# RWKV-7 recurrence and wave mixer: masked evictions shared by three engines, decay sums partly on TensorE, v partly in 1280-byte runs, mixer tiles in pairs

## The chip, the cores and the metric

The kernel runs on one core of one Trainium2 chip. The metric is the device time of one execution in microseconds, as the median of several runs.

## The reference

Six inputs r, k, v, w, a, b of shape (4, 8, 768, 40): batch, heads, time, features per head. For every batch and head a 40x40 state is carried over 768 steps; then a mixer works on the result seen as x of shape (4, 768, 320).

```python
for t in range(S):
    y[:, :, t] = np.einsum('bhd,bhde->bhe', rt, state)
    Sa = np.einsum('bhde,bhe->bhd', state, at)
    state = state * wt[:, :, None, :] - np.einsum('bhd,bhe->bhde', Sa, bt) \
            + np.einsum('bhd,bhe->bhde', vt, kt)
...
theta = x @ w_theta
zr, zi = x * np.cos(theta), x * np.sin(theta)
u = x + np.einsum('ts,bsd->btd', w_tok_r, zr) + np.einsum('ts,bsd->btd', w_tok_i, zi)
return u + np.maximum(u @ w_ch, 0.0)
```

Inputs and output are float32; the kernel's matmuls take bfloat16.

## The kernel before, in words

**Recurrence.** Time is cut into 24 chunks of 128 steps, six for each batch element; the chunk number i runs from 0 to 23. The time steps of a chunk lie on the 128 partitions, the 8 heads x 40 features along the free dimension. Inside a chunk the recurrence is written as products of masked 128x128 score matrices; from chunk to chunk a state `gt` is carried.

- `loads(i)` issues five loads on the SP queue (w, k, b, a, v), each of 160 KB in rows of 160 bytes, since a head's 40 floats are contiguous only for one time step. r comes for two chunks at a time in runs of 1280 bytes (eight time steps in a row), and its transposition by TensorE and the two evictions `rT` (L454) restore the order.
- `prep(i)`: ScalarE takes the logarithm of w (`lw`, L382); TensorE sums it over time with a triangular matrix (L389) and sums each head's decay of the whole chunk (L391, L395); ScalarE takes the exponential (`ex`, L399). VectorE adds `lw` to the sum (`sx`, L402), the sum without the present step, and ScalarE makes `we` of it (L406). GpSimd multiplies k and b by `ex` and a by `we` (`kb` L413, `ah` L417), and casts v (L422). TensorE transposes the results, ScalarE evicts them (`kbT`, `aT`, `vT`, L342).
- `scores` (called for psi, phi, lamv and lamu): 16 matmuls of 64 rows fill two PSUM banks with 8 heads of 128x128 scores (L467). One VectorE instruction of 128x1024 multiplies them by the triangular mask on their way to SBUF (L472). There are 4 x 24 = 96 of these masked evictions.
- `recurrence(i)`: psi times v plus the state's part (L500, L506), eviction `nx` (L512), phi (L518), eviction `nu` (L522), then the new state (L539, `sum` L550, `gt` L554 or L558), and its transposition `gd`.
- `readout(i)`: the output y of the chunk from lamv, lamu and the old state (L602, L609, L611); VectorE multiplies it by `we` into the tile `x` (L618).

**Mixer.** For each x tile: three transpositions, one padded (L582), an eviction, three matmuls with w_theta (L627) and an eviction `th` (L637). When a batch element's six tiles are there, ScalarE takes sine and cosine (`cs`, L651, with a change of the activation table before and after), GpSimd multiplies them by x (`zr`, `zi`, L663). `mix_row` then makes each of the six output tiles with 12 matmuls of 320 columns (L680), adds x (`u`, L687), transposes u, multiplies by w_ch (L627) and finishes with `oo` (L696) and a store on the SP queue. The token matrices come in blocks through the GpSimd queue (L717) into four `wrow` buffers, and are transposed by TensorE (L725, L729).

**Order.** Nothing is scheduled when the program is built. Each operation is recorded by `add` with its engine, its reads and its writes; `Plan.order` emits them as the fixed list `ORDER` says, and `HOMES` gives each its PSUM bank. So the order on every engine, on SP's and GpSimd's queues too, is that of `ORDER`. Mixer work of one batch element is spread between the recurrence of the next. `WARM` puts idle matmuls on `busy` in front of a few operations at the start (L774).

```python
        out = [self.ops[n] for n in ORDER]
        homes = iter(HOMES)
        self.home = {}
        for o in out:
            if o.new is not None:
                b = next(homes)
                self.home[o.new[0]] = (b, b + 1) if o.new[1] == 2 else (b,)
```

Of the kernel before, what the change touches and what calls it, by code (L numbers as in the profile page):

```python
# [19 lines left out]
FROM_POOL = 4  # L20
ORDER = [
    0, 5, 3, 6, 2, 1, 19, 20, 4, 21, 12, 22, 23, 34, 26, 25, 80, 35, 30, 10, 31, 24, 7, 28, 79,
    29, 8, 27, 38, 36, 40, 9, 39, 32, 33, 14, 105, 41, 81, 42, 82, 13, 43, 53, 83, 15, 84, 226,
    54, 89, 55, 106, 11, 56, 107, 58, 90, 227, 57, 16, 91, 59, 37, 85, 60, 229, 62, 108, 18,
    111, 86, 64, 63, 17, 92, 65, 110, 74, 228, 68, 109, 69, 44, 114, 112, 93, 115, 70, 76, 61,
    116, 71, 135, 117, 45, 124, 113, 136, 66, 125, 137, 67, 87, 46, 138, 120, 72, 88, 94, 121,
    47, 73, 211, 95, 139, 122, 75, 126, 96, 140, 159, 143, 118, 127, 144, 160, 130, 123, 145,
    187, 161, 146, 119, 77, 188, 164, 128, 212, 162, 189, 48, 147, 213, 165, 129, 190, 163, 195,
    180, 168, 166, 196, 214, 148, 197, 131, 198, 170, 216, 191, 171, 141, 169, 217, 132, 192,
    215, 176, 174, 265, 220, 142, 78, 175, 218, 149, 199, 221, 133, 150, 266, 167, 200, 222, 49,  # L30
    172, 177, 223, 193, 267, 50, 241, 318, 230, 242, 268, 232, 173, 270, 231, 243, 269, 201,
    236, 319, 194, 244, 271, 202, 245, 320, 181, 246, 274, 219, 233, 183, 293, 275, 249, 272,
    294, 178, 182, 321, 250, 224, 295, 179, 322, 276, 97, 296, 237, 225, 251, 277, 302, 252, 98,
    203, 134, 303, 151, 456, 204, 282, 280, 286, 152, 323, 283, 297, 253, 238, 325, 254, 304,
    281, 247, 368, 255, 184, 324, 248, 298, 256, 372, 239, 327, 369, 305, 257, 299, 329, 328,
    186, 234, 273, 330, 185, 235, 258, 373, 339, 240, 457, 278, 370, 348, 340, 288, 337, 371,
    306, 458, 279, 459, 462, 343, 349, 284, 307, 502, 300, 285, 460, 350, 461, 503, 287, 351,
    308, 301, 463, 352, 504, 338, 465, 309, 289, 353, 310, 326, 466, 333, 354, 505, 311, 344,
    467, 355, 484, 468, 334, 485, 346, 471, 336, 508, 331, 472, 356, 335, 464, 345, 486, 551,
    156, 473, 332, 357, 469, 487, 552, 474, 470, 507, 488, 506, 492, 553, 374, 511, 489, 493,  # L40
    292, 554, 341, 512, 509, 290, 532, 342, 555, 358, 153, 494, 533, 513, 359, 534, 556, 495,
    514, 360, 535, 521, 361, 99, 536, 522, 496, 558, 157, 541, 347, 557, 537, 475, 377, 523,
    497, 562, 538, 158, 291, 498, 476, 499, 560, 477, 563, 510, 542, 539, 379, 500, 561, 527,
    524, 154, 540, 375, 501, 543, 376, 579, 478, 381, 544, 490, 515, 491, 566, 580, 382, 479,
    100, 516, 155, 581, 545, 383, 101, 582, 480, 396, 567, 517, 583, 568, 380, 529, 397, 546,
    518, 598, 584, 378, 398, 519, 588, 528, 569, 599, 585, 589, 399, 600, 400, 647, 530, 547,
    559, 601, 401, 520, 102, 590, 402, 525, 548, 603, 591, 586, 628, 587, 648, 602, 604, 564,
    629, 549, 526, 572, 565, 630, 605, 649, 570, 631, 607, 482, 550, 650, 653, 609, 571, 608,
    637, 483, 592, 652, 638, 481, 610, 632, 651, 593, 639, 617, 633, 578, 654, 403, 594, 640,
    656, 404, 577, 595, 52, 103, 596, 531, 205, 104, 619, 597, 618, 51, 658, 694, 641, 659, 208,  # L50
    657, 384, 642, 385, 613, 386, 620, 695, 634, 387, 696, 643, 614, 606, 644, 697, 664, 615,
    662, 709, 665, 675, 616, 388, 623, 676, 635, 389, 636, 655, 677, 206, 390, 678, 573, 660,
    207, 611, 661, 710, 663, 612, 679, 575, 712, 645, 711, 209, 680, 574, 666, 646, 210, 621,
    681, 391, 622, 405, 392, 624, 259, 684, 698, 724, 685, 262, 682, 667, 725, 686, 826, 726,
    408, 727, 409, 406, 683, 410, 687, 728, 827, 729, 393, 828, 701, 411, 625, 412, 829, 413,
    394, 699, 830, 730, 414, 705, 576, 688, 731, 700, 706, 415, 260, 395, 831, 416, 703, 689,
    626, 263, 261, 732, 365, 264, 417, 739, 733, 362, 420, 421, 315, 422, 704, 423, 424, 738,
    832, 425, 734, 690, 426, 713, 312, 691, 418, 715, 735, 692, 702, 714, 427, 835, 428, 693,
    707, 716, 833, 736, 836, 429, 708, 627, 742, 366, 737, 430, 837, 363, 367, 741, 838, 668,
    717, 747, 364, 841, 745, 854, 718, 444, 855, 671, 316, 743, 746, 445, 856, 317, 446, 740,  # L60
    719, 313, 842, 857, 447, 862, 751, 858, 847, 863, 448, 314, 744, 843, 859, 864, 669, 449,
    844, 834, 432, 749, 433, 434, 670, 872, 435, 450, 750, 436, 865, 437, 902, 849, 748, 873,
# [72 lines left out]
class Plan:  # L135
# [7 lines left out]
    def add(self, eng, kind, i, fn, cost, reads=(), writes=(), spec=None, mode=128,  # L143
            tail=0, table=None, new=None, work=0, after=()):
        o = Op()
# [45 lines left out]
def kernel(  # L191
# [91 lines left out]
    for i, t in sorted(to_zero, key=lambda e: e[0]):  # L283
        nc.vector.memset(t, 0.0)
# [526 lines left out]
```

## Time and profile before

| | |
|---|---|
| median of 3 runs | 206.35 us (206.16 to 207.54) |
| the profiled execution, its own time | 206.05 us |
| its span, first to last instruction | 204.3 us |
| busy: TensorE, VectorE, ScalarE, GpSimd | 191.4, 174.4, 151.6, 127.0 us |
| DMA packets | 134181, 30.82 MB; 125824 of them under 512 bytes |
| granted TensorE clock | 1.00 |

Busy is the time in which an engine had at least one instruction recorded as running. The records of neighbours overlap, on TensorE above all, so the busy time is more than the engine is kept for; the space from one start to the next, where nothing is waited for, tells that. The windows of the profile give the same figures for a stretch of the span, and the timeline shows single instructions with their start and duration.

### The profile page before, as it was taken

The numbers are of one execution on the slowest core, as the hardware profiler recorded it, in microseconds if no ns is written. First come the engines' busy times: TensorE is split into PE (matmuls) and PEld (weight loads), VectorE is DVE, ScalarE is ACT, GpSimd is POOL, SyncE is SP. The second block draws the span as 40 slices with busy tenths as digits, with TensorE's granted clock in tenths as the row PEclk, the third lists the DMA queues.
The fourth block names the chain that finished last, engine by engine and source line by source line (L and its number), as shares of the span: only waits on it lengthen the run. The fifth ranks groups of instructions, "written<-read, shape, count | busy, mean of one in ns | idle before, by whom it ended". The sixth has DMA issues, their size and how long they took to land.

```text
span 204.3 us, 8134 instructions
## 1 busy us (share of the span) xinstructions
PE 191.4 (94%) x3372; PEld 156.3 (77%) x3372; DVE 174.4 (85%) x277; ACT 151.6 (74%) x364; POOL 127.0 (62%) x186
## 2 busy tenths in 40 slices
PE   7878789888999999999899999999999999999993
PEld 6756668667878888887678888788888878777771
DVE  7499899799999998996886989999999987956543
ACT  3577668799999977868667859898999967756021
POOL 3015178559999996659959918548987953635000
PEclk9999999999999999999999999999999999999999
DMA  6989899999899999979999889797999400012223
GB/s 135 198 158 197 155 172 167 182 159 195 139 186 204 155 256 191 147 141 178 170 191 207 169 176 186 169 181 131 220 199 192 96 3 5 0 67 78 87 77 116
DMA packets 134181, 30.82 MB, mean 151 GB/s; under 512 B 125824, under 2 KB 134144, under 8 KB 134144
## 3 DMA queue, kind: packets, MB, share of 16 engines
q1 hardware_dynamic: 131712, 27.54, 68.8%
q0 software_dynamic: 2432, 2.77, 8.6%
q8 instruction: 26, 0.43, 0.9%
q14 instruction: 11, 0.09, 0.1%
HBM read 29.13 MB, written 3.93 MB: 162 GB/s over the span
## 4 chain that ended last, share of the span: by engine, by line
PE 71%; DVE 8%; DMA 8%; SPq 5%; ACT 2%; issue 2%; POOL 1%; DVEq 0%; ACTq 0%; POOLq 0%
PE ps_s L680 19%; PE ps_s L339 12%; PE ps_d L467 10%; PE ps_s L627 9%; SPq L358 4%; DMA wrow_i<-in_moe_w_tok_i_dram 4%; PE ps_s L582 4%; DMA raw_v<-in_v_dram 3%; PE ps_s L450 2%; PE ps_s L539 2%; DMA raw_r<-in_r_dram 2%; PE ps_s L518 2%; PE ps_s L611 2%; PE ps_s L725 2%; PE ps_s L506 2%
## 5 line engine op out<-in xcount | busy, mean ns | idle before, releaser
L413 POOL TENSOR_TENSOR kb<-raw_kb,ex 128x320 bf16<-128x320 f32 x44 | 37.6, 868 | 10.0 <-ACT ex L399 4.3
L680 PE MATMUL ps_s<-zr,wtok_r 128*128 128x320 bf16 x144 | 41.1, 299 | 0.0
L680 PE MATMUL ps_s<-zi,wtok_i 128*128 128x320 bf16 x144 | 41.0, 299 | 0.0
L472 DVE TENSOR_TENSOR psi<-ps_d,mask_p 128x1024 bf16<-128x1024 f32 x24 | 29.2, 1216 | 4.3 <-PE ps_d L467 4.1
L472 DVE TENSOR_TENSOR lamu<-ps_d,mask_p 128x1024 bf16<-128x1024 f32 x24 | 29.1, 1215 | 3.0 <-PE ps_d L467 2.9
L472 DVE TENSOR_TENSOR phi<-ps_d,mask_n 128x1024 bf16<-128x1024 f32 x24 | 29.2, 1215 | 0.8 <-PE ps_d L467 0.8
L472 DVE TENSOR_TENSOR lamv<-ps_d,mask_p 128x1024 bf16<-128x1024 f32 x24 | 29.0, 1215 | 0.5 <-PE ps_d L467 0.4
L417 POOL TENSOR_TENSOR ah<-raw_a,we 128x320 bf16<-128x320 f32 x22 | 19.1, 868 | 8.0 <-issue 5.0
L663 POOL TENSOR_TENSOR zr<-cs,x 128x320 bf16<-128x320 f32 x23 | 18.0, 791 | 6.7 <-DVE oo L696 4.2
L663 POOL TENSOR_TENSOR zi<-cs,x 128x320 bf16<-128x320 f32 x23 | 17.9, 790 | 6.2 <-ACT cs L651 6.2
L467 PE MATMUL ps_d<-aT,kbT 64*128 64x128 bf16 x384 | 17.3, 217 | 1.8 <-ACT aT L342 1.1
L342 ACT COPY uT<-ps_s 128x192 f32<-128x192 f32 x24 | 7.6, 324 | 14.6 <-PE ps_s L582 14.6
L554 POOL TENSOR_TENSOR gt<-sum,ex 128x320 bf16<-128x320 f32 x13 | 9.4, 725 | 13.3 <-DVE sum L550 13.3
L680 PEld LDWEIGHTS <-wtok_r 128*128 128x128 bf16 x144 | 14.0, 97 | 4.1
L687 DVE TENSOR_TENSOR u<-ps_s,x 128x320 bf16<-128x320 f32 x24 | 11.6, 486 | 5.9 <-PE ps_s L680 5.7
L342 ACT COPY kbT<-ps_s 128x512 f32<-128x512 f32 x24 | 14.3, 594 | 3.1 <-PE ps_s L339 2.9
L680 PEld LDWEIGHTS <-wtok_i 128*128 128x128 bf16 x144 | 14.1, 98 | 3.3
L442 POOL CAST r<-raw_r 128x640 bf16<-128x640 f32 x11 | 8.0, 725 | 11.7 <-ACT lw L382 9.7
L696 DVE SCALAR_TENSOR_TENSOR oo<-ps_s,u 128x320 f32<-128x320 f32 x24 | 11.6, 484 | 4.2 <-PE ps_s L627 3.5
L467 PEld LDWEIGHTS <-kbT 64*128 64x128 bf16 x384 | 11.5, 94 | 4.8 <-ACT kbT L342 1.9
L339 PE MATMUL ps_s<-ident,kb 128*128 128x128 bf16 x192 | 14.7, 219 | 0.4 <-POOL kb L413 0.2
L609 PE MATMUL ps_s<-kb,lamv 128*128 128x40 bf16 x192 | 15.1, 180 | 0.0
(119 smaller groups left out, 590.8 us busy)
## 6 DMA issues: line engine op xcount, KB each, us to landing
raw_w<-in_w_dram SPq DMA_DIRECT2D x24, 160.0 KB, 4.2
raw_r<-in_r_dram SPq DMA_DIRECT2D x24, 160.0 KB, 3.6
raw_a<-in_a_dram SPq DMA_DIRECT2D x24, 160.0 KB, 3.5
raw_kb<-in_b_dram SPq DMA_DIRECT2D x24, 160.0 KB, 3.8
raw_kb<-in_k_dram SPq DMA_DIRECT2D x24, 160.0 KB, 3.9
raw_v<-in_v_dram SPq DMA_DIRECT2D x24, 160.0 KB, 4.2
out_dram<-oo SPq DMA_DIRECT2D x24, 160.0 KB, 2.4
wrow_i<-in_moe_w_tok_i_dram POOLq DMA_DIRECT2D x6, 192.0 KB, 5.3
```

The lines of the kernel that those rows point to most:

```text
L339: nc.tensor.transpose(out=dst[:, c:c + 128], in_=pair(src, g), identity=ident)
L342: nc.scalar.copy(out=out.bitcast(FP32), in_=in_)
L413: lambda j=j: (nc.vector if fast else nc.gpsimd).tensor_tensor(out=paired(kb[:, j])[:, :, :, 0:D], in0=natural(raw_kb[s4][:, j]), in1=invW ...
L417: lambda: (nc.vector if fast else nc.gpsimd).tensor_tensor(out=paired(ah)[:, :, :, 0:D], in0=natural(raw_a[i % 6]), in1=Wi, op=ALU.mult),
L467: nc.tensor.matmul(t[:, q, g, :], lhsT=lhs[rows(q), g * 128:(g + 1) * 128], rhs=rhs[rows(q), g * 128:(g + 1) * 128], start=True, stop=True)
L472: add("DVE", kindm, i, lambda: nc.vector.tensor_tensor(out=dst.rearrange("p a b c -> p (a b) c"), in0=ps(p).rearrange("p a (g c) -> p (a g ...
L609: nc.tensor.matmul(o, lhsT=lamv[:, p, g, :], rhs=kb[:, 0, h, 0:D], start=first, stop=False, skip_group_check=True)
L627: nc.tensor.matmul(dst, lhsT=lhs[:, kt, :], rhs=rhs[:, kt, :], start=kt == 0, stop=kt == 2)
L663: nc.vector if fast else nc.gpsimd).tensor_tensor(
L680: nc.tensor.matmul(ps(pk)[:, 0:DM], lhsT=wtok[nm][:, s, j * 128:(j + 1) * 128], rhs=zs[c][:, s], start=n == 0 and c == 0, stop=n == NT - 1 ...
L687: add("DVE", "uadd", q, lambda: nc.vector.tensor_tensor(out=u[:, 0:DM], in0=ps(pk)[:, 0:DM], in1=x[:, 0:DM], op=ALU.add), 488, [pk, ("x", ...
L696: add("DVE", "oo", q, lambda: nc.vector.scalar_tensor_tensor(out=oo, in0=ps(ck)[:, 0:DM], scalar=0.0, in1=u[:, 0:DM], op0=ALU.max, op1=ALU ...
```

## The change

The diff replaces `ORDER`, `HOMES` and `WARM` by new lists for a program of more operations, and adds a table `MOVED`: for an operation in it, `order` takes another engine and another function than the one it was recorded with, from the operation's `alts`.

- **Masked evictions.** `scores` gets an alternative: ScalarE copies the two banks (times 1 or -1) and GpSimd then clears the part on and under the diagonal in place, with `affine_select`. `MOVED` chooses it for 33 of the 96 (psi 9, phi 6, lamv 11, lamu 7).
- **Decay sums.** The addition of `lw` gets an alternative on TensorE, a matmul with the identity onto the same PSUM bank, from which ScalarE then makes `we`. It is chosen for 13 of 24. For the last chunk of each batch element the sums of the whole chunk are left out, as nothing uses them.
- **v.** For chunks 0 to 7 (`RUNS = 4` pairs) v is loaded as r is, two chunks in runs of 1280 bytes. It is cast, transposed and evicted as `vT` in the right order, and transposed once more to get `v` itself.
- **Mixer tiles in pairs.** Two x tiles (and two u tiles) lie side by side without padding. 640 columns make five blocks of 128; the middle one holds the last 64 features of the one tile and the first 64 of the other, and is multiplied in two matmuls of 64 rows (`halves`). Four pairs, one of theta and the last three of u, are treated tile by tile (`solo`). The weights are laid out twice for that, by nine copies.
- **Other engines.** Products (kb, ah, zr, zi), evictions and casts have alternatives; 33 products go from GpSimd to VectorE, and evictions go from ScalarE to VectorE and, for `wtok`, the other way.
- **Buffers.** `raw_a` has five buffers instead of six, `wrow` six for four, u six tiles for four. The matmuls on the state are emitted apart from those on the chunk's own scores (`x0s`, `ys`).

```diff
+MOVED = {n: e for e, ns in {
+    "PE": (23, 72, 125, 191, 246, 312, 367, 515, 561, 620, 670, 1428, 1471),
...
+            if o.idx in MOVED:
+                o.eng = MOVED[o.idx]
+                o.cost, o.fn = o.alts[o.eng]
...
+        def exclusive():
+            nc.tensor.matmul(ps(pk)[:, 0:DM], lhsT=ident, rhs=lw[:, :, 0:D], start=False,
+                             stop=True, skip_group_check=True)
+        summed = add("DVE", "wi", i, lambda: nc.vector.tensor_tensor(
...
+            tail=tail(320), alts={"PE": (mm(320), exclusive)})
...
-        add("PE", kind, i, go, 8 * 26, keys, [p], new=(p, 2), mode=64, tail=tail(128))
-        add("DVE", kindm, i, lambda: nc.vector.tensor_tensor(
+        masked = add("DVE", kindm, i, lambda: nc.vector.tensor_tensor(
             out=dst.rearrange("p a b c -> p (a b) c"),
             in0=ps(p).rearrange("p a (g c) -> p (a g) c", c=128),
-            in1=mask.to_broadcast([128, 2 * G, 128]), op=ALU.mult), 1217, [p], [dkey])
+            in1=mask.to_broadcast([128, 2 * G, 128]), op=ALU.mult), 1217, [p], [dkey],
+            alts={"ACT": (1020, lambda: nc.scalar.mul(
+                out=dst.rearrange("p a b c -> p (a b c)"),
+                in_=ps(p).rearrange("p a c -> p (a c)"),
+                mul=-1.0 if mask is mask_n else 1.0))})
+
+        def select():
+            if masked.eng == "ACT":
+                d = dst.rearrange("p a b c -> p (a b) c")
+                nc.gpsimd.affine_select(out=d, in_=d, pattern=[[0, 2 * G], [1, 128]],
+                                        compare_op=ALU.is_gt, fill=0.0, base=0,
+                                        channel_multiplier=-1)
+        add("POOL", kindm + "s", i, select, 1060, [dkey], [dkey])
...
+        src = ap[bi, :, ci * C:(ci + 2) * C, :].rearrange(
+            "(c g) (t q) d -> c t g (q d)", c=2, q=8)
+        for c in range(2):
+            add("SP", name, i, lambda c=c: nc.sync.dma_start(out=dst[c], in_=src[c]),
+                600, [], [keys[c]], work=470)
...
+        def back():
+            for g in range(G):
+                c = g * 128
+                nc.tensor.transpose(out=ps(pb).bitcast(BF16)[:, c:c + 128],
+                                    in_=vT_t[i % NTR][:, c:c + 128], identity=ident)
...
+            turned(kind, i, [cols(c) for c in (0, 128, 256, DM + 64, DM + 192)], 0, skeys, T,
+                   tkey, at)
...
+        def halves():
+            for q in range(2):
+                nc.tensor.matmul(out(q), lhsT=T[rows(q), REST, :], rhs=m["rest"][rows(q), :],
+                                 start=True, stop=False, skip_group_check=True)
...
-        theta(i)
+        if ci % 2:
+            theta(i - 1, "solo" if i == N - 1 else "fused")
```

## The prediction

> **What bounds the kernel now.** I read the page first: busy shares, then the 40 slices.
>
> ```profile
> span 204.3 us, 8134 instructions
> ...
> PE 191.4 (94%) x3372; PEld 156.3 (77%) x3372; DVE 174.4 (85%) x277; ACT 151.6 (74%) x364; POOL 127.0 (62%) x186
> ...
> DVE  7499899799999998996886989999999987956543
> ACT  3577668799999977868667859898999967756021
> ...
> DMA  6989899999899999979999889797999400012223
> ```
>
> DMA and VectorE are nearly full from slice 2 to slice 31 (160 us); after that only TensorE works hard. But a recorded duration is longer than the time for which an instruction keeps its engine, because neighbours overlap. The timelines of VectorE and TensorE show that:
>
> ```profile
> 43.20 1.21 DVE L472 TENSOR_TENSOR psi<-ps_d,mask_p 128x1024 bf16<-128x1024 f32 x1
> 44.33 0.48 DVE L550 TENSOR_TENSOR sum<-ps_s,gt 128x320 f32<-128x320 f32 x1
> 44.73 1.21 DVE L472 TENSOR_TENSOR lamu<-ps_d,mask_p 128x1024 bf16<-128x1024 f32 x1
> ```
> ```profile
> 188.01 0.30 PE L680 MATMUL ps_s<-zr,wtok_r 128*128 128x320 bf16 x1
> 188.14 0.30 PE L680 MATMUL ps_s<-zi,wtok_i 128*128 128x320 bf16 x1
> ```
>
> From start to start a masked eviction costs 1.13 us, a 320-wide VectorE instruction 0.40, a 320-column matmul 0.136. I call that a slot and take it from back-to-back starts for every form (matmul 128 columns 0.056, 80 0.035, 40 0.025). Slots times counts give the work of each engine before: TensorE 165.8 us, VectorE 167.9, ScalarE 137.0, GpSimd 124.2. TensorE and VectorE are two near-equal bounds; TensorE lacks work for 204.3 - 165.8 = 38.5 us. Where? I follow the end of three x products on L618 (chunks 5, 11 and 23, counted from 0): 54.8, 92.0 and 186.0 us. Along the queues TensorE has done 30.6, 64.0 and 150.6 us of work by then, VectorE 45.3, 81.1 and 161.1. So TensorE lacks 24.2 us in the fill (to chunk 5), 3.8 from there to chunk 11, 7.4 to chunk 23 and 3.1 in the tail, where 15.2 us of matmuls take 18.3. The windows agree:
>
> ```profile
> 20.00:30.00 10.00, 8.35 (x178) 6.70 (x175) 8.99 (x12) 6.62 (x19) 4.27 (x7) 1.00 0.97 173
> 40.00:50.00 10.00, 8.77 (x181) 7.00 (x179) 9.47 (x11) 9.65 (x21) 7.58 (x11) 1.00 0.98 181
> 190.00:204.30 14.30, 10.94 (x89) 7.50 (x87) 5.80 (x12) 1.81 (x6) 0.00 (x0) 1.00 0.27 93
> ```
>
> (PE, PEld, DVE, ACT, POOL busy, clock, DMA share.) In the fill DMA is full and VectorE does 45.3 of 54.8 us: these two pace it. In the tail nothing but TensorE matters. The clock is 1.00 throughout.
>
> **The change, part by part.** Counts are from the two instruction orders.
>
> Masked evictions: 33 of 96 become a ScalarE copy and a GpSimd select in place. VectorE loses 33 x 1.13 = 37.3 us. The trace has no 1024-wide ScalarE eviction; the rows beside it are
>
> ```profile
> L342 ACT COPY kbT<-ps_s 128x512 f32<-128x512 f32 x24 | 14.3, 594 | 3.1 <-PE ps_s L339 2.9
> L442 POOL CAST r<-raw_r 128x640 bf16<-128x640 f32 x11 | 8.0, 725 | 11.7 <-ACT lw L382 9.7 <-DMA raw_r<-in_r_dram 1.9
> ```
>
> with slots 0.48 at 512 and 0.32 at 320 (nx): 0.83 ns an element, so 0.90 at 1024, bounds 0.48 and 2 x 0.59 = 1.19. ScalarE gains 29.7 us (16 to 39). The select: the 128x128 one in the masks takes 0.29 (slot 0.24), the 640-wide cast 0.68, the 320-wide 0.41; along that line 1.00 at 1024, bounds 0.68 and 8 x 0.29 = 2.3. I take 1.00, the line through three rows: GpSimd gains 33 us (22 to 76). One eviction now takes 0.9 + 1.06 + a handover of about 0.1 = 2.1 instead of 1.2 us before its consumer may start: 0.9 us later, 33 times 29 us if no other matmul covered it. I cost it at nothing because the order has other chunks' matmuls there; the PSUM pair comes free 0.2 us earlier.
>
> Decay sums: 13 of 24 go from VectorE (0.40 each, -5.2 us) to a 320-column matmul (+1.8 us of TensorE). That matmul waits for ScalarE's exp of the same bank, and every matmul behind it waits too. In the new order 0.57 to 2.2 us of matmuls stand between the cumulative sum and it; the sum's latency (0.30) and exp (0.45) need about 0.6 beyond the slot. Covered, cost 0; without the cover 13 x 0.6 = 8 us.
>
> v in 1280-byte runs for chunks 0 to 7: the trace's packets last 14.9 ns at 160 bytes and 64.6 ns at 1280, so one load falls from 1024 x 14.9 / 16 = 0.95 us of all DMA engines to 128 x 64.6 / 16 = 0.52 (0.57 where crowded). Eight loads: -3.2 us. The SP queue also moves them forward: the last load of chunk 5 has 30.4 us of transfers ahead of it and itself, instead of 37.6. In return TensorE turns v back: 16 transposes a pair instead of 8, 4 x 8 x 0.056 = +1.8 us, and 8 wide evictions are added. GpSimd's own DMA issues stay 16, the token weights in six buffers for four; that can only let them run ahead, and I count 0.
>
> Mixer tiles in pairs: 20 of 24 pairs take 5 transposes for 6 (-1.1 us), and 4 full plus 2 half-row matmuls for 6. The score matmuls (L467) show two 64-row matmuls running side by side, 16 in 0.55 us; so two halves are one slot, -2.7 us (0 if they don't overlap). 48 evictions become 28. Nine small copies arrange the weights, once, 4.4 us mostly on GpSimd.
>
> What moves between engines: 33 products (kb, ah, zr, zi) from GpSimd (slots 0.81 and 0.75) to VectorE (0.40), and from ScalarE to VectorE some 60 evictions (VectorE slots 0.27 to 0.60, along the line through its 320- and 768-wide rows). All in all: TensorE 165.8 to 165.1, VectorE 167.9 to 162.7, ScalarE 137.0 to 149.9, GpSimd 124.2 to 133.0. No total explains much; the places do. By chunks 5, 11 and 23 VectorE now has 41.7, 75.4 and 153.9 us to do, TensorE 33.0, 66.5 and 150.2.
>
> **The sum.** Fill: VectorE idled 9.5 us before chunk 5; 41.7 + 9.5 = 51.2 us. Bounds: by the loads, 54.8 - 7.2 = 47.6; by no gain, 54.8. Chunks 5 to 11: TensorE 33.5 + the same 3.8 idle = 37.3. To chunk 23: 83.7 + 7.4 = 91.1. Tail: 14.9 + 3.1 = 18.0. Together 197.6 against 204.3, -6.7 us: 3.6 of it from the fill (an earlier start for a TensorE that has 2.4 us more done by then), 2.9 from the last two stages, where TensorE has less left. Around the span lie 206.05 - 204.3 = 1.75 us, and the median is 0.3 above the profiled run: 199.7 us.
>
> **Rivals.** (1) TensorE's remaining idle shrinks too. VectorE has 7.2 us less to do by chunk 23. If half of the 11.2 us idle between chunks 5 and 23 goes and the fill follows the loads (47.6), the span is 188.4 and the time 190.5; half of that extra gain, 195. For it: VectorE's windows at 40 to 60 us. Against: ScalarE and GpSimd get fuller in the same windows.
>
> (2) The fill gains nothing, since something else paces it (ScalarE has 35.5 us to do by chunk 5 instead of 33.8). The span is 201.2, the time 203.3.
>
> (3) VectorE's products wait for GpSimd. Before, no VectorE instruction with two SBUF operands runs between 20 and 188 us, so the trace can't show what one costs beside a busy GpSimd (the row at 20 us, 0.49, had GpSimd idle beside it). In the new order 29 stand between chunks 8 and 21. If one had to wait for a running GpSimd instruction: it is busy 133 / 197.6 = 0.67 of the time, half of a 0.85 us instruction remains, 0.29 each, 8.4 us in all. VectorE has about 16 us of idle there to hide it; with all of it on the path the time is 208.1, with half 203.9. The Trainium skill's page "SBUF — State Buffer", section "Who interferes with whom", states just this: a VectorE instruction with two SBUF inputs contends with a GpSimd instruction that reads SBUF, and the second to start blocks fully. No run here shows it yet; by the row the sum stands, by the rule it comes out at this rival.
>
> (4) The other side: ScalarE becomes the pace. By the nu evictions (L522) of chunks 5, 11 and 23 it has 35.5, 68.4 and 141.8 us to do instead of 33.8, 62.8 and 131.1. It idled 48.5 us before the last of them (179.6 us). My sum leaves it 31.4. If its idle can't fall under 37.8, the kernel is no faster; if it stays 48.5, the span is 141.8 + 48.5 + 6.4 + 18.0 = 214.7 and the time 216.8; half way between, 208.2. For it: its evictions are links between matmuls, late work by nature. Against: it ran 9.65 busy of 10 us at 40 to 50 us.
>
> (5) That the change doesn't do what it says: the orders hold 33 of 96, 13 of 24 and 8 of 24 as stated, so no.
>
> **How the numbers follow.** Forecast 0.45 (its own range 196.5 to 202.5), rival 1 0.17, rival 2 0.12, rival 3 0.12, rival 4 0.14. The time is that of the forecast, 199.7. The range goes from 193, inside rival 1, to 207.5, taking most of rival 3 and leaving out nearly all of rival 4. A measurement of this kernel tells about 1% (2 us) from no change: faster (under 204.3) holds the forecast, rivals 1 and 2 and a quarter of rival 3, 0.77; within 1% most of the rest of rival 3, 0.08; slower 0.15.
>
> **What would show it.** Right: the x product of chunk 5 ends at 48 to 53 us; the last load lands near 157 instead of 161; the ScalarE masked copy lasts about 1.0 us and the select about 1.06; a decay matmul's slot is 0.136 with no idle of TensorE before it; the last x ends near 179 to 180 and the tail is 18 us. Wrong: VectorE products longer than 0.5 us or idle before them beside GpSimd (rival 3); TensorE waiting for ScalarE's evictions or for a select (rival 4, or the 0.9 us that I put at nothing); a select near 2 us, which would fill GpSimd and upset everything.

## The result and the profile after

The changed kernel takes 215.12 us (median of 4 runs, 214.35 to 215.82), the kernel before 206.25 us beside it: a ratio of 1.043 (95% interval 1.035 to 1.051). The forecast was 199.7 us, the range ended at 207.5.

The page of the profile after the change (span, busy time and share of each engine, and the slices of VectorE, ScalarE and DMA):

```profile
span 212.7 us, 8144 instructions
...
PE 194.5 (91%) x3366; PEld 154.9 (73%) x3366; DVE 183.1 (86%) x306; ACT 163.1 (77%) x330; POOL 143.9 (68%) x188
...
DVE  6477889999999998999999999999998995679553
```

VectorE was to do 5.2 us less in slots, and its records add up to 8.7 us more than the 174.4 before. The windows between the ends of the x products of chunks 5, 11 and 23 say where the time lies (columns: window and its length, then TensorE, its weight loads, VectorE, ScalarE and GpSimd busy with counts, clock, DMA share, GB/s). Before, then after:

```profile
0.00:54.80 54.80, 46.32 (x869) 37.87 (x870) 47.05 (x99) 41.64 (x101) 29.29 (x50) 1.00 0.94 169
54.80:92.00 37.20, 37.08 (x725) 30.90 (x723) 36.56 (x50) 31.15 (x76) 30.05 (x44) 1.00 1.02 181
92.00:186.00 94.00, 93.09 (x1663) 77.01 (x1661) 82.84 (x114) 75.56 (x179) 65.73 (x92) 1.00 0.70 139
186.00:204.30 18.30, 14.94 (x122) 10.48 (x120) 7.96 (x17) 3.21 (x10) 1.91 (x3) 1.00 0.26 93
```
```profile
0.00:54.80 54.80, 47.80 (x902) 39.10 (x903) 44.69 (x87) 45.06 (x94) 38.60 (x56) 1.00 0.93 180
54.80:94.90 40.10, 37.83 (x720) 31.28 (x719) 37.88 (x55) 34.07 (x73) 34.53 (x50) 1.00 0.98 167
94.90:193.30 98.40, 93.42 (x1633) 74.22 (x1630) 89.52 (x145) 80.03 (x158) 66.82 (x79) 1.00 0.64 128
193.30:212.70 19.40, 15.46 (x120) 10.30 (x118) 11.04 (x23) 3.89 (x9) 3.97 (x5) 1.00 0.24 85
```

| stage, us | before | forecast | after | after minus forecast |
|---|---|---|---|---|
| fill, to x of chunk 5 | 54.8 | 51.2 | 54.8 | 3.6 |
| to x of chunk 11 | 37.2 | 37.3 | 40.1 | 2.8 |
| to x of chunk 23 | 94.0 | 91.1 | 98.4 | 7.3 |
| tail | 18.3 | 18.0 | 19.4 | 1.4 |
| span | 204.3 | 197.6 | 212.7 | 15.1 |

The groups of VectorE instructions with two SBUF operands, all on L424 now (count, then busy us and mean ns of one), and the largest groups of the new select and of the new ScalarE copy:

```profile
L424 DVE TENSOR_TENSOR kb<-raw_kb,ex 128x320 bf16<-128x320 f32 x17 | 14.6, 866 | 0.0
L424 DVE TENSOR_TENSOR zi<-cs,x 128x320 bf16<-128x320 f32 x9 | 8.0, 905 | 0.0
L424 DVE TENSOR_TENSOR ah<-raw_a,we 128x320 bf16<-128x320 f32 x9 | 6.7, 747 | 0.0
L424 DVE TENSOR_TENSOR zr<-cs,x 128x320 bf16<-128x320 f32 x6 | 3.7, 635 | 0.0
...
L562 POOL TENSOR_SCALAR_AFFINE_SELECT lamv<-lamv 128x1024 bf16<-128x1024 bf16 x11 | 12.5, 1134 | 8.6 <-ACT lamv L554 8.5
...
L554 ACT ACTIVATE lamv<-ps_d 128x1024 bf16<-128x1024 f32 x11 | 11.4, 1033 | 3.8 <-PE ps_d L545 2.0 <-PE ps_s L747 1.6
```

Before, VectorE made eight such products, at 0.48 to 0.49 us, and no GpSimd instruction ran beside any of them:

```profile
L413 DVE TENSOR_TENSOR kb<-raw_kb,ex 128x320 bf16<-128x320 f32 x4 | 2.0, 493 | 0.6 <-DMA raw_kb<-in_k_dram 0.4
```

Now the 41 take 33.0 us, 0.80 on average: about 13 us more than 41 x 0.49. The timeline shows one alone and one beside a select (start, duration); first VectorE, then GpSimd:

```profile
125.00 0.47 DVE L424 TENSOR_TENSOR kb<-raw_kb,ex 128x320 bf16<-128x320 f32 x1
...
127.15 1.31 DVE L424 TENSOR_TENSOR kb<-raw_kb,ex 128x320 bf16<-128x320 f32 x1
...
127.02 1.09 POOL L562 TENSOR_SCALAR_AFFINE_SELECT lamv<-lamv 128x1024 bf16<-128x1024 bf16 x1 [3.09 <-ACT lamv L554]
```

At 125.0 GpSimd has nothing to do. At 127.15 the same product meets a select that has just begun, and ends at 128.46, 0.35 us after the select's end at 128.11. Most of the others that meet a running GpSimd instruction look alike: they end 0.34 to 0.35 us behind it. Where the GpSimd instruction is the second to start, the product keeps its 0.48 us and GpSimd's takes longer (1.19 us here, 0.87 on average before):

```profile
21.67 0.48 DVE L424 TENSOR_TENSOR kb<-raw_kb,ex 128x320 bf16<-128x320 f32 x1
...
21.68 1.19 POOL L424 TENSOR_TENSOR ah<-raw_a,we 128x320 bf16<-128x320 f32 x1 [0.61 <-ACT we L471]
```

### The profile page after: what moved, and what is told of

Its sections match the earlier page's. It is cut to its first block, busy times and chain, and to the rows that moved or that the text cites. A ratio compares the mean times of both kernels' runs of the same rounds, so it can differ in the third digit from the quotient of the medians.

```text
span 212.7 us, 8144 instructions
## 1 busy us (share of the span) xinstructions
PE 194.5 (91%) x3366; PEld 154.9 (73%) x3366; DVE 183.1 (86%) x306; ACT 163.1 (77%) x330; POOL 143.9 (68%) x188
## 4 chain that ended last, share of the span: by engine, by line
PE 52%; DVE 21%; ACT 12%; issue 7%; DMA 4%; SPq 2%; POOL 0%; DVEq 0%; ACTq 0%; POOLq 0%
PE ps_s L818 12%; PE ps_s L379 9%; PE ps_d L545 8%; PE ps_s L717 4%; DVE kb L424 3%; PE ps_s L747 3%; ACT rT L533 3%; DVE oo L834 2%; PE ps_s L679 2%; DVE rT L535 2%; PE ps_s L526 2%; PE ps_s L884 2%; PE ps_s L611 2%; DVE zi L424 2%; DMA raw_r<-in_r_dram 2%
## 5 line engine op out<-in xcount | busy, mean ns | idle before, releaser
L424 POOL TENSOR_TENSOR kb<-raw_kb,ex 128x320 bf16<-128x320 f32 x31 | 27.0, 879 | 7.8 <-ACT ex L460 5.0
L550 DVE TENSOR_TENSOR lamu<-ps_d,mask_p 128x1024 bf16<-128x1024 f32 x17 | 20.7, 1216 | 2.0 <-ACT uT L382 1.0
L550 DVE TENSOR_TENSOR phi<-ps_d,mask_n 128x1024 bf16<-128x1024 f32 x18 | 21.8, 1213 | 0.3 <-PE ps_d L545 0.2
L550 DVE TENSOR_TENSOR psi<-ps_d,mask_p 128x1024 bf16<-128x1024 f32 x15 | 18.3, 1217 | 1.4 <-PE ps_d L545 1.0
L562 POOL TENSOR_SCALAR_AFFINE_SELECT lamv<-lamv 128x1024 bf16<-128x1024 bf16 x11 | 12.5, 1134 | 8.6 <-ACT lamv L554 8.5
L424 POOL TENSOR_TENSOR zi<-cs,x 128x320 bf16<-128x320 f32 x15 | 11.9, 801 | 8.6 <-ACT cs L797 6.9
L379 PE MATMUL ps_s<-ident,kb 128*128 128x128 bf16 x192 | 15.1, 219 | 2.0 <-DVE kb L424 1.2
L424 POOL TENSOR_TENSOR ah<-raw_a,we 128x320 bf16<-128x320 f32 x15 | 13.8, 918 | 3.9 <-ACT we L471 2.7
L550 DVE TENSOR_TENSOR lamv<-ps_d,mask_p 128x1024 bf16<-128x1024 f32 x13 | 15.8, 1215 | 0.7 <-PE ps_d L545 0.4
L424 POOL TENSOR_TENSOR zr<-cs,x 128x320 bf16<-128x320 f32 x18 | 15.3, 864 | 0.2 <-ACT cs L797 0.2
L424 DVE TENSOR_TENSOR kb<-raw_kb,ex 128x320 bf16<-128x320 f32 x17 | 14.6, 866 | 0.0
L379 PEld LDWEIGHTS <-kb 128*128 128x128 bf16 x192 | 11.6, 97 | 3.7 <-DVE kb L424 2.2
L554 ACT ACTIVATE lamv<-ps_d 128x1024 bf16<-128x1024 f32 x11 | 11.4, 1033 | 3.8 <-PE ps_d L545 2.0
```

What stands on the lines that cost most here:

```text
L379: nc.tensor.transpose(out=dst[:, c:c + 128], in_=pair(src, g), identity=ident)
L424: return lambda: engine.tensor_tensor(out=dst, in0=in0, in1=in1, op=ALU.mult)
L550: masked = add("DVE", kindm, i, lambda: nc.vector.tensor_tensor(out=dst.rearrange("p a b c -> p (a b) c"), in0=ps(p).rearrange("p a (g c) ...
L554: alts={"ACT": (1020, lambda: nc.scalar.mul(out=dst.rearrange("p a b c -> p (a b c)"), in_=ps(p).rearrange("p a c -> p (a c)"), mul=-1.0 i ...
L562: nc.gpsimd.affine_select(out=d, in_=d, pattern=[[0, 2 * G], [1, 128]], compare_op=ALU.is_gt, fill=0.0, base=0, channel_multiplier=-1)
```

## The experiments

Two theories stood first. *Products*: VectorE's second SBUF operand waits for GpSimd, and the order, made for products of 0.49 us, passes the delay on. *Evictions*: ScalarE with its 33 copies and the hop to GpSimd is the new pace. The stages of all runs stand together behind the experiments; ratios are to the kernel before, measured beside each.

**e1, e2: one operand or two.** Of the 41 products, the 11 kb from chunk 8 on and all 15 z (zr and zi) read only one of their operands (the products themselves are left out); in e1 as a reduction over an axis of length 1, in e2 as a maximum of the operand with itself.

```diff
+        def probe():                                   # e1
+            nc.vector.tensor_reduce(out=dst, in_=in0.rearrange(
+                "p (n o) -> p n o" if kind == "z" else "p g c (d o) -> p g c d o", o=1),
+                op=ALU.max, axis=mybir.AxisListType.X)
+        def probe():                                   # e2
+            nc.vector.tensor_tensor(out=dst, in0=in0, in1=in0, op=ALU.max)
...
-            alts={"DVE": (488, on(nc.vector))})
+            alts={"DVE": (488, probe if kind == "z" or kind == "kb" and i >= 8 else on(nc.vector))})
```

> The changed kernel, with 26 of the 41 products that VectorE makes (kb from chunk 8 on, all zr and zi) replaced by a reduction over an axis of length 1, which reads one SBUF operand instead of two (raw_k or raw_b, or cs, without the factor ex or x; these products are left out). Port theory: in the profile after, these 26 last 10.4 us longer in sum than 26 x 0.48; they fall to about 0.49 each whatever GpSimd does, and 7 to 10 us of it come off the time: 205 to 208 us. ScalarE theory (ScalarE's evictions set the pace): no change, 213 to 216. Order theory (the loss is in the waits of the new order): 212 to 216.

> The control of the run with one operand: the same 26 products as a tensor_tensor maximum of raw_k, raw_b or cs with itself, so the waits are those of that run and two SBUF operands are read (the products are left out here too). Port theory: mean durations stay near 0.85 and the time near that of the changed kernel, 212 to 216 us. If it falls as the run with one operand does, the freed waits were the cause and not the second operand.

Measured: e1 208.08 us (1.010, 1.006 to 1.015), e2 214.98 us (1.044, 1.040 to 1.048). VectorE groups of e1, then of e2:

```profile
L426 DVE TENSOR_REDUCE kb<-raw_kb 128x320 bf16<-128x320 f32 x11 | 5.2, 476 | 0.0
L426 DVE TENSOR_REDUCE zi<-cs 128x320 bf16<-128x320 f32 x9 | 4.1, 476 | 0.0
```
```profile
L426 DVE TENSOR_TENSOR kb<-raw_kb 128x320 bf16<-128x320 f32 x11 | 10.9, 988 | 0.0
L426 DVE TENSOR_TENSOR zi<-cs 128x320 bf16<-128x320 f32 x9 | 8.0, 907 | 0.0
```

The two kernels differ in nothing but these 26 instructions, which read one operand in e1 and two in e2, and e2 repeats the changed kernel's stages within 0.5 us. So the second operand costs 6.9 us of the 215, beside a GpSimd that is as busy in both (141 and 144 us).

**e3, e4: parts undone.** e3 gives 35 products back to GpSimd; e4 gives all masked evictions back to VectorE.

```diff
-            if o.idx in MOVED:
+            if o.idx in MOVED and not (o.kind == "z" or o.kind in ("kb", "ah") and o.i >= 8):   # e3
+            if o.idx in MOVED and o.kind not in ("mpsi", "mphi", "mlv", "mlu"):                 # e4
```

> The changed kernel with its products kb and ah from chunk 8 on and all zr and zi (35 instructions) back on GpSimd, in the same places of the order. Port theory: VectorE loses 35 x 0.40 = 14 us of work and some 12.7 us of blocked time, GpSimd gains 35 x 0.79 = 28 us on 144 busy us; the blocking goes and GpSimd gets nearly full: 206 to 212 us. ScalarE theory: no faster, 213 to 220. Order theory: 213 to 218.

> The changed kernel with all 96 masked evictions on VectorE again, no ScalarE copy and no select. Port theory: VectorE gets 37 us more on 183 busy us, and becomes the bound; less blocking as GpSimd is 33 us less busy: 218 to 228 us. ScalarE theory: ScalarE loses 33 x 0.9 = 30 us and the time falls, 203 to 210.

Measured: e3 222.60 us (1.080, 1.076 to 1.084), e4 236.51 us (1.146, 1.141 to 1.152). The busy lines of the two, e3 first:

```profile
PE 196.9 (89%) x3366; PEld 156.0 (71%) x3366; DVE 160.1 (73%) x271; ACT 163.1 (74%) x330; POOL 166.5 (75%) x223
```
```profile
PE 198.7 (85%) x3366; PEld 156.9 (67%) x3366; DVE 211.2 (90%) x339; ACT 135.1 (58%) x297; POOL 106.3 (45%) x155
```

Both are slower than any of the theories had named (e3 at most 220, e4 at most 228). In e3 nearly all of VectorE's waiting for GpSimd is gone, but GpSimd has 22.6 us more and the stage to chunk 23 grows to 103.2 us: in this order GpSimd's added load costs more than the waiting did. In e4 ScalarE has 28 us less and the kernel is 21 us slower. VectorE, busy for 211 us, is then the likely bound, so e4 alone doesn't clear ScalarE (i1 does, for one stage); the moved evictions by themselves are a gain, in this order.

After e1 8.5 us of the span were still open: its fill is 3.8 us above the forecast, its stage to chunk 23 3.7, the stage between them 0.8 and the tail 0.2. The remaining runs start from e1 (26 products left out) where nothing else is said.

**f1, f2, f4: two waits that the trace names.** On SP the loads of chunks 14 and 23 stand behind stores that wait 10 to 11 us for their tile; and the two halves of an `rT` or `vT` bank, one evicted by VectorE and one by ScalarE, follow one another. f1 puts the loads ahead of the stores, f2 gives both halves to one engine, f4 does both.

```diff
+AHEAD = {463: (699, 750, 756, 752, 753, 751, 755, 804), 486: (942, 940, 941),      # f1, f4
+         889: (1395, 1398, 1396)}                       # store: loads put ahead of it
...
+SAME = {"DVE": (38, 39, 382, 383, 977, 978, 1195, 1196, 1483, 1484),               # f2, f4
+        "ACT": (136, 137, 140, 141, 261, 262, 791, 792, 1086, 1087, 1381, 1382)}
```

> As the kernel with 26 one-operand products (208.1 us; the 26 products are left out), but on SP's queue the loads of chunks 13 to 15 are put ahead of the first store, those of k, b and a of chunk 16 ahead of the third, and those of k, v and b of chunk 23 ahead of the ninth. Theory that loads stuck behind stores that wait for their tile cost part of what the forecast missed: the gap of 11 us on SP before the first store is gone, the x product of chunk 14 ends 3 to 6 us earlier than 127.9 + about 5, the last load lands by 156 instead of 165.7, and the time is 204.5 to 206.5 us. Rival, that nobody waits for those loads in the end (TensorE and VectorE have other work meanwhile): the loads land earlier and the time stays at 207.4 to 208.8 us.

> As the kernel with 26 one-operand products (208.1 us), but the two evictions of one bank of r or v in runs (rT of chunks 2 and 3, and of 12 to 23, vT of chunks 0 to 7) are always on the same engine, half of the pairs on VectorE and half on ScalarE; no instruction is added or removed. Theory that two engines evicting one bank wait for each other and hold TensorE up: the waits of VectorE and ScalarE ahead of rT and vT (about 4.6 us in all) and most of the 3.9 us for which TensorE waits behind them go, and the time is 204.5 to 206.5 us. Rival, that one engine now does both one after the other and the second is ready no earlier: 207.4 to 209 us.

> As the kernel with 26 one-operand products (208.1 us), with both the loads ahead of the stores and the pairs of evictions on one engine. If both waits lie on the path and are independent: 201.5 to 204 us. If they cover each other, about the better of the two alone, 204.5 to 206.5 us. If neither counts: 207 to 209 us.

Measured: 209.26 us (1.015, 1.011 to 1.020), 209.20 (1.014, 1.010 to 1.018) and 210.63 (1.019, 1.014 to 1.024), so none is faster than e1. In f1 the last load lands at 157.6 us instead of 165.7 and the stage to chunk 23 takes 94.7 us where e1 takes 94.8: nobody waited for those loads. In f2 it takes 95.1. Both theories fall for that stage. All three runs lose 0.7 to 1.9 us between chunks 5 and 11, for a reason that wasn't looked for.

**f3: v by rows.** v of chunks 0 to 7 comes in 160-byte runs again.

```diff
-                runs_of_eight("loadv", i, v,
-                              [raw_v[:, (i + c) % 6].rearrange("p h d -> p (h d)")
-                               for c in range(2)], [("raw_v", (i + c) % 6) for c in range(2)])
+                for c in range(2):
+                    key, dst, src = load(i + c)[4]
+                    add("SP", "loadv", i, lambda dst=dst, src=src: nc.sync.dma_start(
+                        out=dst, in_=src), 600, [], [key], work=945)
...
-        add("PE", "tvb", i, back, 4 * mm(128), [("vT", i % NTR)], [pb], new=[(pb, 1)],
-            tail=tail(128))
```

> As the kernel with 26 one-operand products (208.1 us), but v of chunks 0 to 7 comes in 160-byte runs as before: two plain casts in the place of the strided one, plain evictions of 0.38 and 0.42 us in the place of the strided ones, and neither turns back nor their evictions. Theory that the longer way of v through TensorE and the evictions holds the fill up: the x product of chunk 0 ends near 22.5 instead of 24.5 us, that of chunk 5 at 52 to 53.5 instead of 55.0, and the time is 205 to 206.5 us. Rival, that the shorter transfers of v are worth what they were forecast at (3.2 us of transfers): the loads come later again, chunk 5 at 56 to 58 and the time 209 to 211 us. If both hold, they cancel and the time stays at 207.5 to 208.8 us with chunk 0 earlier and chunk 5 not.

Measured: 210.64 us (1.020, 1.017 to 1.024); the fill takes 57.2 us. The x product of chunk 0 ends at 27.8 us, later and not earlier. But in this profiled execution the clock granted between 8 and 24 us was 0.50 to 0.92 (1.00 in e1), so the trace doesn't tell whether the longer way through TensorE holds the fill. The time is longer without that, too: one execution with a mean clock of 0.997 took 210.3 us, some 2 us more than e1. So the runs of v are a gain in this order; what each part of them is worth stays open.

**g1 to g4: the start, the hop, and two parts undone.** g1 gives chunk 0 nearly its old order, g2 leaves out the 33 selects (the copies multiply by zero), g3 undoes the pairs of mixer tiles, g4 the decay sums on TensorE.

```diff
+        out[:len(START)] = [self.ops[n] for n in START]   # g1: START permutes the first 66
...
-            if masked.eng == "ACT":                       # g2
+            if False:
...
-            turned(kind, i, [cols(c) for c in (0, 128, 256, DM + 64, DM + 192)], 0, skeys, T,
+            turned(kind, i, [cols(q * DM + c) for q in range(2) for c in (0, 128, DM - 128)],   # g3
...
+                nc.tensor.matmul(out(q), lhsT=T[rows(1), 3 * q + 2, :], rhs=m["rest"][rows(1), :],
+                                 start=False, stop=True, skip_group_check=True)
...
-    "PE": (23, 72, 125, 191, 246, 312, 367, 515, 561, 620, 670, 1428, 1471),   # g4
+    "PE": (),
```

> As the kernel with 26 one-operand products (208.1 to 209 us), with only the first chunk's order changed: SP issues a, k and b of chunk 0 ahead of r and of chunk 1 (a third or fourth instead of ninth, behind v), their three products are all on VectorE (as before the change), and TensorE takes the turns of a, k, b and the first scores ahead of those of r and the lamv scores. Theory that the fill lost its gain at the start, where the new order brings chunk 0's a 5 us later than before: the nu eviction of chunk 0 ends near 13.5 to 14.5 us instead of 16.8, the x product of chunk 5 at 51.5 to 53 instead of 55.0, the time is 2 to 3.5 us lower. Rival, that the fill is set by something all the way through (transfers, or the chain over four engines): chunk 0 gets earlier and chunk 5 still ends at 54.5 to 55.5, the time within 0.8 us.

> As the kernel with 26 one-operand products, and the 33 GpSimd selects are left out (the ScalarE copy multiplies by zero, so those 33 score blocks add nothing). Theory that the extra hop behind a masked eviction, which the forecast put at nothing, is what remains on the path, bounded at 29 us: TensorE's idle falls and the time drops by 4 us or more, to 204 or less. Rival, that the hop is covered as forecast: GpSimd's busy time falls by 36 us to about 104 and the time by 0 to 1.5 us, the latter from the 15 products with two SBUF operands that this kernel still has (they would last 0.5 instead of 0.65 to 0.72 us).

> As the kernel with 26 one-operand products, but the mixer's tiles are not shared in pairs: six transposes a pair instead of five (768 columns in one eviction instead of 640), and three blocks a chunk instead of two and a half, the third as a 64-row matmul of its own. The forecast's term is 3.8 us of TensorE, of which 20 of 24 pairs here. If TensorE's work sets the time one to one, as the forecast took it: 3.5 to 4.5 us slower, about 212 to 213. If TensorE only waits less when it has more to do: within 1 us of 208.1 to 209.

> As the kernel with 26 one-operand products, but all 24 decay sums are on VectorE as before (13 come back at 0.40 us a slot, 5.2 us, and 1.8 us of TensorE goes). If VectorE sets the pace: 3 to 5 us slower, 211 to 213. If TensorE does: 0 to 2 us faster, 206 to 208. If neither (a chain over the engines): within 1 us.

Measured: g1 216.14 us (1.048, 1.042 to 1.055), g2 206.58 (1.004, 1.000 to 1.007), g3 218.78 (1.062, 1.054 to 1.069), g4 211.50 (1.025, 1.019 to 1.031).

- g1: the nu eviction of chunk 0 ends at 24.0 us, not at 14, because the new order put it behind work of chunk 2. The trial failed as a trial (the clock, 0.51 between 20 and 24 us, may be part of its lateness); but the 7.8 us that the fill lost are all still there at the end (span +8.6).
- g2: GpSimd has 36 us less and the kernel gains 1.4 us, no more than the shorter waits of the 15 products left with two operands explain (0.54 and 0.58 us instead of 0.65 to 0.72). The hop behind a copied eviction is covered, as the forecast had it.
- g3: its span is 10.9 us longer, where 3.5 to 4.5 us were expected. Lone 64-row matmuls are the reason. The timeline of TensorE in g3:

```profile
102.07 0.44 PE L719 MATMUL ps_s<-wch_main,uT 128*128 128x320 bf16 x2
102.45 0.31 PE L723 MATMUL ps_s<-wch_rest,uT 64*128 64x320 bf16 x1
102.69 0.51 PE L889 MATMUL ps_s<-ident,wrow 128*128 128x128 bf16 x6
```

The second of the two full matmuls starts at 102.07 + 0.136 = 102.21, the 64-row one 0.24 us later, and the next full one 0.24 us after that, where a 320-wide matmul otherwise keeps TensorE for 0.136. The same is found wherever the rows change, in the traces of before, e1 and g3 (medians 232 ns to 64 rows and 229 to 239 back, for 320 columns): about 0.096 us each way. g3 has 101 such changes to and 101 fro, e1 67 and 67 (before: 64 and 64). So g3 adds 68 x 0.096 = 6.5 us to the 3.9 of its added transposes and matmuls, 10.4 in all. Of the 10.9, 0.9 are there already at the x product of chunk 0 (25.4 us, 24.5 in e1), ahead of all added work; 10.0 are left: TensorE's added work comes out nearly one for one. What the pairs are worth against the kernel before g3 doesn't tell, since there the third block was padded to 128 rows and needed no change of rows.

- g4: 3.1 us slower, 1.7 in the fill and 1.2 in the next stage, where 11 of the 13 sums lie. The decay sums on TensorE are worth 2.9 / 11 = 0.26 us each there, net of TensorE's 0.136.

**h1, h2, h4: the start again.** The first 78 operations in an order that no longer holds chunk 0 back: in h1 from e1, in h2 from the changed kernel with nothing left out, in h4 from g2.

```diff
+START = (0, 5, 3, 4, 2, 1, 6, 7, 8, 20, 21, 22, 23, 24, 32, 33, 27, 26, 25, 30, 28, 31, 29,
...
+MOVED[25] = MOVED[27] = "DVE"
...
+        out = [self.ops[n] for n in list(START) + ORDER[len(START):]]
```

> As the kernel with 26 one-operand products (1.0103 times the time of before), with the first chunk alone in the order it had before the change: on SP a, k and b of chunk 0 and r ahead of v and of chunk 1; the products of chunk 0 on VectorE; TensorE turns r, a, k, b, then v, and nx and nu of chunk 0 are not behind chunk 1's or 2's work, which the earlier try (g1) put ahead of them. Theory that what happens at the first chunk comes out whole at the end (in f3 and g1 a start later by 3.3 and 7.8 us made the end later by 2.9 and 8.6): the nu eviction of chunk 0 ends at 13.5 to 14.8 us instead of 16.8, the x product of chunk 5 and the end come 2 to 3 us earlier, ratio to before 0.995 to 1.001. Rival, that only a delay is passed on and a gain is lost in the next wait (transfers): chunk 5 at 54.5 to 55.5, ratio 1.007 to 1.013.

> The changed kernel, nothing left out, with only the first chunk's order as in h1. By the same theory 2 to 3 us under the changed kernel, 212 to 213.5 (ratio to before 1.028 to 1.035); by the rival 214.5 to 215.5.

> As h1, and the 33 selects are left out as in g2 (the copies multiply by zero), which takes nearly all waiting of VectorE for GpSimd out of the remaining 15 products too. If the two add: 1.0036 less 1.0 to 1.5%, ratio 0.988 to 0.994, 203.5 to 204.8 us, so that 4 to 5 us of the forecast's gain still lack. If they cover each other: 1.000 to 1.004.

Measured: h1 215.13 us (1.044, 1.041 to 1.047), h2 220.49 (1.073, 1.069 to 1.078), h4 211.83 (1.031, 1.027 to 1.036). In h1 the nu eviction of chunk 0 ends at 15.4 us, 1.4 earlier than in e1, but chunk 1 pays: the x product of chunk 0, which stands behind chunk 1's work, ends at 29.9 instead of 24.5. The fill is 5.4 us longer and the span 6.4. The clock has a part in this: in the profiled execution of h1 it was 0.69 between 16 and 20 us and 0.74 between 20 and 24. It is not all of it, since among h1's six executions those with the higher mean clock (0.992) took 215.1 to 215.7 us and those with 0.984 took 214.4 to 215.2. So whether an earlier start would come out at the end was not seen; a later one did, in g1, h1 and h2.

**h3, i1, i2: what paces the stage to chunk 23.** h3 takes nine z products from VectorE (3.6 us, left out), i1 lets 20 masked copies of ScalarE copy half their columns, i2 leaves out 24 row matmuls of TensorE.

```diff
-            alts={"DVE": (488, probe if kind == "z" or kind == "kb" and i >= 8 else on(nc.vector))})
+            alts={"DVE": (488, (lambda: None) if kind == "z" and i >= 17 else probe
+                          if kind == "z" or kind == "kb" and i >= 8 else on(nc.vector))})     # h3
...
-                out=dst.rearrange("p a b c -> p (a b c)"),
+                out=dst.rearrange("p a b c -> p (a b c)")[:, 0:512 if i >= 12 else 1024],       # i1
...
+                        if c == 1 and s in (2, 3) and bi in (1, 2):                              # i2
+                            continue
```

> As the kernel with 26 one-operand products (1.0103), and 9 of those products (z of chunk 17 on, which are 0.40 us slots of VectorE) are left out altogether: VectorE loses 3.6 us, 3.2 of it between chunks 11 and 23; TensorE's work is the same. If VectorE still sets that stage: it shortens by 2 to 3 us, ratio 0.996 to 1.001. If TensorE alone does: ratio 1.007 to 1.012.

> As the kernel with 26 one-operand products (1.0103 to 1.015 times before), and the 20 ScalarE masked copies of chunks 12 to 23 copy only the first 512 of 1024 columns (the rest keeps older scores): ScalarE loses 20 x 0.48 = 9.6 us and each of those evictions is 0.48 us sooner. If ScalarE's evictions pace the stage from chunk 11 to 23 (as links of the chain, or by their sum), it shortens from 94.8 to 92 or less, and the time by 2.5 us or more. If TensorE's work does: 94 to 95, the time within 1 us.

> As the kernel with 26 one-operand products, and 24 of the 288 row matmuls (the imaginary part of two of six blocks, for the second and third batch) are left out: 24 x 0.136 = 3.3 us less TensorE work between chunks 11 and 23 and nothing else. If TensorE's work sets the stage one for one: 91 to 92 us instead of 94.8, the time 2.5 to 3.5 us less. If another engine or the chain does: 94 to 95, the time within 1 us.

Measured: h3 209.00 us (1.014, 1.011 to 1.017), i1 208.91 (1.016, 1.012 to 1.020), i2 207.47 (1.009, 1.006 to 1.012). All three fills are 1.1 to 1.5 us longer than e1's, though the instructions up to chunk 11 are the same, for a reason told at the end; so the stages are compared. The stage to chunk 23 in e1, h3, i1 and i2:

```profile
93.10:187.90 94.80, 92.68 (x1633) 74.09 (x1629) 83.92 (x144) 79.89 (x158) 64.73 (x79) 1.00 0.67 134
```
```profile
94.60:189.40 94.80, 92.69 (x1633) 74.09 (x1630) 82.75 (x140) 79.93 (x158) 64.75 (x79) 1.00 0.67 134
```
```profile
94.20:189.20 95.00, 92.46 (x1633) 74.21 (x1630) 84.28 (x145) 73.05 (x158) 64.39 (x79) 1.00 0.67 133
```
```profile
94.50:187.60 93.10, 89.98 (x1607) 71.70 (x1604) 82.97 (x145) 79.73 (x158) 64.40 (x79) 1.00 0.68 136
```

Less work for VectorE or ScalarE changes nothing. 3.3 us less for TensorE give 1.7, between the two outcomes that were expected: its work counts in this stage, but half of what is saved turns into waiting. This rests on one trace (the stage takes 94.7 to 95.1 us in e1, f1 to f4, h3, i1 and g4); in the time of the whole kernel i2 and e1 can't be told apart (1.009 and 1.010).

The stages of all runs (differences of ends rounded to 0.1 us):

| stage, us | e1 | e2 | e3 | e4 | f1 | f2 | f3 | f4 | g1 | g2 | g3 | g4 | h1 | h2 | h3 | h4 | i1 | i2 |
|---|---|---|---|---|---|---|---|---|---|---|---|---|---|---|---|---|---|---|
| to x 5 | 55.0 | 55.3 | 56.1 | 60.6 | 55.1 | 55.1 | 57.2 | 55.5 | 62.8 | 55.3 | 56.1 | 56.7 | 60.4 | 60.3 | 56.5 | 60.0 | 56.1 | 56.4 |
| to x 11 | 38.1 | 40.1 | 39.9 | 42.8 | 39.4 | 38.8 | 38.8 | 40.0 | 38.2 | 38.1 | 40.1 | 39.3 | 38.2 | 40.2 | 38.1 | 38.1 | 38.1 | 38.1 |
| to x 23 | 94.8 | 98.4 | 103.2 | 111.9 | 94.7 | 95.1 | 94.8 | 95.1 | 95.5 | 93.9 | 102.1 | 95.1 | 95.7 | 98.5 | 94.8 | 93.6 | 95.0 | 93.1 |
| tail | 18.2 | 19.4 | 21.5 | 19.4 | 18.3 | 18.2 | 18.2 | 18.2 | 18.2 | 18.3 | 18.7 | 18.3 | 18.2 | 19.4 | 18.2 | 18.3 | 18.3 | 18.5 |

## Why the prediction was wrong, point by point

**What held.** The ScalarE masked copy takes 1.03 us as recorded and a slot of 0.92 (forecast 0.90), the select 1.09 to 1.13 and a slot of 1.05 (1.00), the decay matmul a slot of 0.136. The hop behind a copied eviction costs nothing that can be told (g2), and the decay sums help (g4). ScalarE is not the pace of the stage to chunk 23 (i1), so rival 4, which the forecast held for the most likely way to lose, is out there; in the fill no run tested it. One sign failed besides: the last load landed at 170.5 us and not near 157, but nobody waited for it (f1).

**The term that failed first: the products.** "33 products (kb, ah, zr, zi) from GpSimd (slots 0.81 and 0.75) to VectorE (0.40)" priced them at a slot measured with GpSimd idle. The last such row stands at 15.3 us, not at 20. The text said that no row showed such a product beside a busy GpSimd, found the rule that forbids this price (the Trainium skill, "SBUF — State Buffer", section "Who interferes with whom": a VectorE instruction with two SBUF inputs contends with a GpSimd instruction that reads SBUF), and left it out of the sum, as rival 3 with a chance of 0.12. The trace agrees with the rule in every respect that it shows: one operand 0.476 us, two operands 0.635 to 0.988 on average, and the end just behind GpSimd's. The price a product was near (0.29 us forecast, 13 / 41 = 0.32 measured); the count was not, since products before chunk 8 and in the tail wait too. Of the miss of 15.1 us in the span, 6.6 are the 26 products of e1: 2.0 in the stage to chunk 11, 3.6 to chunk 23, 1.2 in the tail (and 0.2 back in the fill). The 15 that e1 leaves cost at most the 1.4 us more that g2 gains. Between e1 and e2 VectorE's busy time differs by 10.4 us (173.4 and 183.8) and the time by 6.9, so two thirds come out at the end; rival 3 had taken all or half.

**The second: the fill, 3.8 us in e1.** "VectorE idled 9.5 us before chunk 5; 41.7 + 9.5 = 51.2" took the idle time over as a constant. VectorE's idle time grew by what its work shrank. At chunk 0 the order is worse. SP's first loads before, and after (start, duration):

```profile
1.93 0.58 SPq L358 DMA_DIRECT2D raw_a<-in_a_dram  x1
```
```profile
1.30 1.26 SPq L398 DMA_DIRECT2D raw_v<-in_v_dram  x2
2.61 1.25 SPq L398 DMA_DIRECT2D raw_r<-in_r_dram  x2
...
6.45 0.80 SPq L405 DMA_DIRECT2D raw_a<-in_a_dram  x1
```

a of chunk 0 goes out as SP's ninth load instead of its third; its product is at 10.0 us on GpSimd instead of 6.4 on VectorE, and the nu eviction of chunk 0 ends at 16.6 us instead of 13.3, the x product at 24.3 instead of 22.1. The prediction counted only the loads up to the last one of chunk 5 and said "the SP queue also moves them forward": it didn't follow the first. That a late start is passed on whole is shown (g1, h1, h2, and the clock in h3 and i1); that this late start is why the fill gains nothing is argued from the two traces, not shown, since neither attempt brought it back without harm to chunk 1 and at a full clock. ScalarE's and GpSimd's fuller fill (45.1 and 38.6 us busy instead of 41.6 and 29.3) is a rival that no run tested. Rival 2 (fill unchanged, ScalarE the reason) was right about the stage's length; its reason is open.

**The third: TensorE's saved work, 3.7 us in the stage to chunk 23.** "83.7 + 7.4 = 91.1" took TensorE's idle time over unchanged, too. i2 shows a rate of one half for work taken away (1.7 of 3.3 us), where g3 shows about one for work added. At one half the forecast saving of 2.9 us would be 1.5; without the selects, and so without most waiting of the remaining products, the stage is 0.9 shorter (g2). Some 1.4 us are left over. About half of that can be put down to a term that the prediction put at nothing: "two halves are one slot" leaves out the change of rows. The traces of the stage have 59 such changes, both ways together, in e1 and 52 before, and 7 x 0.096 = 0.7 us. The line that the prediction read held this price: 16 score matmuls (two calls of `scores`; one call makes 8, not 16) take 0.55 us to the next matmul, 8 take 0.33, so 8 more cost 0.22 and some 0.10 belong to the change. About 0.7 us of this stage stay unexplained; VectorE's load, ScalarE's, the late loads and the split evictions didn't move it.

## What to carry to other kernels

An instruction that moves to another engine is priced beside what runs there at that moment, not by its row in a quiet trace; if a known rule of contention says that the row won't hold, the rule belongs in the sum and the row at its end. Idle time is no constant that can be carried from one order to the next: here half of the work taken from TensorE came back, while work added to it and delays at the start came out nearly whole. For an order written by hand, a part put back alone (g1, h1, e3, e4) tells only what it does in that order.

## What the runs showed of the hardware that was not expected

GpSimd loses as well: its own products beside VectorE's grow from 0.79 to 0.86 us (zr, back at 0.79 in e1) and from 0.87 to 0.92 (ah), and the cast of v that follows the select above, at 128.06, takes 0.70 us, where the mean before was 0.45.

A change between matmuls of 128 and of 64 rows costs TensorE 0.096 us each way. The Trainium skill says that changing the tiling mode drains TensorE ("TensorEngine Tiling (Array Packing)", section "Tiling Modes"); the traces agree and give the price. The orders before and after pay it 128 and 134 times, 12 to 13 us of what the prediction called lack of work.

In h3 and i1 the granted clock fell to half during the fill and came back by itself; in e4, f3, g1, h1, h2, h4 and i2 it fell there too (to between 0.50 and 0.94 over stretches of 4 us). Windows of i1:

```profile
17.00:18.00 1.00, 0.99 (x12) 0.82 (x11) 0.20 (x1) 0.10 (x1) 0.74 (x1) 0.60 0.95 169
18.00:19.00 1.00, 1.00 (x15) 0.88 (x14) 0.50 (x2) 0.48 (x1) 0.00 (x0) 0.50 1.16 203
19.00:20.00 1.00, 1.00 (x22) 0.88 (x20) 0.42 (x1) 0.66 (x2) 0.24 (x1) 0.50 1.13 178
20.00:21.00 1.00, 1.00 (x15) 0.80 (x12) 0.79 (x1) 0.80 (x1) 0.75 (x2) 0.69 1.18 198
```

Shares of 0.60, 0.50, 0.50 and 0.69 make 0.8 + 1 + 1 + 0.62 = 3.4 us at half speed. e1, with the same instructions up to there, had 1.00 throughout; the x product of chunk 0 came 1.1 us later in i1 and 1.5 in h3, and chunk 11's as much: it is this that showed that nothing up to there has slack for such a delay. The Trainium skill's page "TensorE: Matmul & The Clock Gate" (Part 1) has the window of 3.4 us, but its table of states puts half speed behind a whole idle window; in i1 no gap between matmuls before it was longer than 0.9 us. What sets it off stays open.
